# A searched instruction order for chunk-selected attention with a gated MLP: a new order, zero products moved to the front, loads moved, and two gate tiles transposed by TensorE

## The chip, the core and the metric

The kernel runs on one core of one Trainium2 chip. The metric is the device time of one execution in microseconds (us). The engines are TensorE (PE, with its weight loads shown apart as PEld), VectorE (DVE), ScalarE (ACT), GpSimd (POOL) and SyncE (SP). In this kernel POOL issues all loads from memory, and SP issues all other DMAs: copies inside the chip's memory, transpositions by DMA, and the stores of the output.

## The reference

For each of 4 batches and 8 heads (768 positions, head size 64), each query picks at most 6 of 24 key chunks of 32 by an upper bound, attends to those causally, and the result goes through a gated MLP. Cut to what is computed:

```python
k_min, k_max = k_chunks.min(axis=3), k_chunks.max(axis=3)
ub  = sum(maximum(q * k_min, q * k_max), -1)          # bound of each query with each chunk
sel = the 6 chunks with the largest ub among the causal ones
scores = where(sel & causal, q @ k.T / 8, -1e9)
x   = softmax(scores) @ v                             # heads side by side: [4, 768, 512]
h   = relu(x @ w_in);  u, v = h[..., :512], h[..., 512:]
v_n = (v - mean(v)) / sqrt(var(v) + 1e-6)
out = (u * (w_spatial @ v_n + b_spatial)) @ w_out
```

## The kernel before

**Tiles and stages.** Positions are six tiles of 128. Two heads make a pair: pairs 0 to 15, four to a batch. Two pairs make a group, 0 to 7, which is what one load of K, Q or V covers. For each pair the kernel transposes keys and queries on PE, reduces the keys to chunk bounds on DVE, multiplies bounds with the positive and negative parts of the queries, takes the 8 largest per query and head, and writes the mask of what is not selected beside the queries. Queries and mask are transposed together, so that one product gives masked scores. ACT takes the exponential, PE multiplies with V, DVE divides by the sum. When a batch's four pairs are done its MLP runs, and PE mixes its products with the attention of the next batch. After the last pair only the MLP of batch 3 is left.

**The order.** Every piece of work has a name. One long string, `ORDER` (L379 on), lists all 1446 names, and the kernel's last loop emits them in that order. Each engine runs its own pieces in the order in which they are emitted and waits where an operand or a buffer is not ready. The string came from a planner in the same file (`Sim` and `build`), which has a cost and a priority for each piece; it isn't run when the kernel is, except that `build(PLAN)` says which engine takes which piece. `PLAN['flip']` lists pieces that go to the other of ACT and DVE.

**Names used below.** With `i` a pair, `g` a group, `h` one of two heads and `b`,`t` a batch and a token tile:

- `dz`, `dm0` to `dm64`: a cleared tile (L564) and 65 products of it with itself (L868), which nobody reads; they keep PE busy while the first data is on its way.
- `ring0` to `ring3`: clearing of the query buffers (L527); `id0`, `id1`: the identity matrix (L523, L524); `kh..`: clearing halves of the key operands (L569).
- `lk`, `lq`, `lv` with g and h: loads of K, Q, V (L584, L590, L595; group 0 by head and pair, L599); `win`, `wsp`, `wout`, `lb`: MLP weights (L603 to L622).
- `kT`, `qT`: transposes of keys and queries (L660, L717); `kTb0`, `kTb1`, `qTb0`: a second copy of them for the first pairs; `kc`: the copy of a transposed key out of PSUM (L698); `kop`: the key operand, a copy by DVE or ACT, and from pair 8 on a DMA on SP (L710).
- `kmax`, `kmin`, `kb`: key bounds (L681, L703); `rq`: query parts (L726, L728); `ub`: the bounds' product; `top`, `sel`: selection (L747, L773).
- `aT`, `ac`: transposes of query and mask on PE and their copy (L792, L795); from pair 8 on `aTd` does this by DMA on SP (L798).
- `sc`, `ex`, `tri`, `av`, `rc`, `nm`: scores (L805), exponentials (L814), the causal triangle on POOL (L820), values product (L831), reciprocal (L836) and division (L841); `x`, `xp`: transposition of the result, from pair 4 on by DMA (L850).
- MLP: `v`, `u`, `s`, `o` products (L925, in halves `.0`, `.2`, `.4`), `va`, `ua` relus, `bs`, `vs`, `rs`, `vn` the normalisation, `gt` the gate (L968), `gd` its transposition by DMA (L974), `oc` the copy of an output tile out of PSUM (L979), `os` its store (L983).

**What sets the order around the change.** `av000` needs `lv0`; `qT2` needs `lq10` and `lq11`. A score needs `aT`/`aTd` and `kop` of its pair. An output tile `o` needs the transposed gate tile of `gd`. PSUM has three banks for scores, three for MLP products, and one each for transposes (`tr`) and values.

The lines of the transposition by DMA are

```python
st["gT", ti] = ml.tile([P, KO, P], F16, tag="gT", name="gT", bufs=NQT)
nc.sync.dma_start_transpose(out=st["gT", ti], in_=st["g", ti])
```

Of the kernel before, what the change touches and what calls it, by code (L numbers as in the profile page):

```python
# [59 lines left out]
class Sim:  # L60
# [10 lines left out]
    def run(s,fixed=None):  # L71
# [16 lines left out]
        warm=getattr(s,'warm0',0.) or 1e9; touch={}  # L88
# [8 lines left out]
        while n<N:  # L97
# [68 lines left out]
def mmc(n): return max(n/2.4+2.5,25)/1000  # L166
DEF=dict(BEATS=12,pa=8,dve_a=(),qx=('ACT',),xp=4,mlp_first=13,mlp_mul=1.0,sc=3,tr=1,acc=1,ml=3,kbuf=3,qbuf=3,vbuf=3,ebuf=3,late=240,chunk=2,
  lk=40,lq=36,lv=18,kdma=99,kcp=2,kcdma=1,kc_act=(),shift=4,prep=0.0,tm=0.0,lm=0.0,head=1,lag=0.0,kp=27,ca=99,tree=0,svk=1.4,svw=1.15,flip=(),wide=0,pt=(),xd=(),dum=0,warm0=0.,qa_dve=(),ma_act=(),mkbuf=2)
PEL=0.2
def build(prm=None):  # L170
# [24 lines left out]
    for g in range(1,8):  # L195
        t0=2*g*BE
        for hi in range(2):
            op(f'lk{g}{hi}','POOL',1.007,acq=[('k',g)],prio=t0-p['lk']+hi,dma=(p['svk'],1.9+p['lm']))
            op(f'lq{g}{hi}','POOL',1.007,acq=[('qs',g)],deps=[f'ring{g}'] if g<p['qbuf'] else [],prio=t0-p['lq']+hi,dma=(p['svk'],1.9+p['lm']))
        op(f'lv{g}','POOL',1.41,acq=[('v',g)],prio=t0-p['lv'],dma=(2*p['svk'],1.9+p['lm']),deps=['small'])  # L200
# [120 lines left out]
    for b in range(B):  # L321
# [29 lines left out]
        for ti in range(NQT):  # L351
            op(f'vn{b}{ti}','DVE',.457,.09,deps=[f'rs{b}'],acq=[('vn',b)],uses=[('vraw',b)],prio=pri[last('u',b,ti,4)]+.6)
            q=pri[last('s',b,ti,6)]
            op(f'gt{b}{ti}','DVE',.66,.09,deps=[last('s',b,ti,6),f'ua{b}{ti}','lb'],acq=[('g',f'{b}{ti}')],uses=[('ml',f's{b}{ti}'),('u',b)],prio=q+.5)
            op(f'gd{b}{ti}','SP',1.22,deps=[f'gt{b}{ti}'],acq=[('gT',f'{b}{ti}')],uses=[('g',f'{b}{ti}')],prio=q+.7,dma=(.82,1.5+p['tm']))
# [21 lines left out]
PLAN = {'late': 40, 'mlp_first': 8, 'qbuf': 4, 'kbuf': 4, 'vbuf': 4, 'dum': 65, 'warm0': 6.5, 'kcp': 8, 'flip': ['ac11', 'ac20', 'ac60', 'kc11', 'kc9', 'kh11', 'kh20', 'kh21', 'kh30', 'oc00', 'oc02', 'oc11', 'oc13', 'oc14', 'oc15', 'oc22', 'oc24']}  # L377

ORDER = """  # L379
ring3 lk010 ring1 dz lq010 ring0 dm13 dm14 dm55 dm31 dm7 id0 dm11 ring2 lk000 dm59 dm53 dm20 dm27 dm4 small dm46 dm42  # L380
dm23 lq000 dm1 dm50 dm60 dm61 dm35 dm22 dm25 id1 dm40 dm47 dm63 lk011 dm39 expand lk001 kh20 kh00 kh21 lq001 kh30 kT0
kh11 dm57 dm3 dm52 dm64 kTb0 kmin0 lq011 dm8 dm36 qT0 kop01 dm30 qTb0 rq00 lk10 dm5 dm9 dm6 dm28 dm15 dm24 kmax0 rq01
dm10 dm37 dm41 dm26 dm48 dm18 dm19 dm43 dm21 dm51 dm33 mlat kop00 kT1 kb0 lk11 dm17 dm45 kmax1 kh31 kTb1 lv0 dm58 ub0
kmin1 dm32 kop11 dm38 dm0 dm44 dm54 dm12 dm62 qT1 dm34 dm29 top00 kh10 mtri rq11 kh01 top01 lq11 selA0 kb1 aTA00 sel0
kop10 dm16 rq10 dm56 dm2 aTB0 lq10 acA00 ub1 acB0 aTA01 sc000 top10 lk20 sc001 ex000 dm49 acA01 kT2 top11 sc002 ex001
win11 sc010 kop20 ex002 sc003 win30 kop21 ex010 av000 sel1 lq21 sc004 ex003 kmax2 sc005 aT11 ex004 sc011 win31 kmin2
aT10 ex005 ex011 lq20 av001 sc013 ac10 av002 ac11 sc015 sc012 rc00 lk21 qT2 kb2 ex013 nm00 qT3 ex015 kT3 rq20 ex012
sc100 win10 rq21 sc102 ex100 av010 rq30 lk30 sc014 kmax3 ex102 sc101 ub2 ex014 lq30 sc103 kmin3 ex101 av011 sc111
ex103 lv1 av012 top20 sc112 ex111 sc105 rc01 top21 ex112 sc104 nm01 ex105 lk31 sc114 ex104 kb3 rq31 sc113 av100 sel2
ex113 sc110 win21 kop31 aT20 ex114 kop30 ub3 win20 aT21 ex110 ac20 av101 sc115 top30 av102 ex115 sc200 ac21 sc203  # L390
top31 lq31 sc201 rc10 sel3 kT4 ex200 nm10 qT4 ex203 lq40 sc204 kmax4 av110 ex201 sc202 ex204 av111 kmin4 sc215 aT30
win01 ex202 xp0 sc205 ex215 rq40 sc211 ac30 kb4 sc210 kop40 av112 lv2 ex205 ex211 rq41 sc212 kop41 ex210 ub4 sc213 x0
ex212 kT5 rc11 sc214 top40 ex213 sc300 ex214 nm11 aT31 sc301 top41 ex300 av200 lq41 kop50 ex301 av201 sc305 sel4 sc302
ac31 kmin5 av202 qT5 win00 xp1 ex305 ex302 sc310 rq50 sc303 lk40 rc20 ex310 rq51 sc304 nm20 ex303 aT40 sc311 kmax5
wsp0 ex304 av210 sc315 ex311 av211 kop51 sc312 ac40 av212 x1 kT6 ex312 rc21 sc313 kb5 nm21 aT41 ex315 ex313 kmax6
sc405 xp2 ac41 av300 sc314 x2 av301 ex405 sc404 ex314 kmin6 sc400 ub5 ex404 sc401 av302 top50 ex400 sc403 kT7 rc30
ex401 top51 sc402 ex403 sel5 nm30 aT50 ex402 sc415 kmax7 av310 ac50 sc411 tri40 av311 sc412 kb6 ex415 kop61 qT6 ex411
wsp2 av312 sc413 ex412 rq60 sc410 wsp3 rc31 ex413 rq61 sc501 wsp4 nm31 ex410 aT51 wsp5 sc503 kop60 av400 ac51 lk50
kmin7 sc414 xp3 ex501 ub6 x3 av401 ex503 sc502 av402 top60 ex414 v00.0 rc40 ex502 sc504 kb7 nm40 v00.2 tri41 ex504
sc505 top61 sc500 av410 ex505 wsp1 sel6 ex500 sc511 av411 kop70 qT7 lv5 sc514 kop71 av412 sc510 ex514 rq70 v02.0 rq71  # L400
va00 v01.0 lk41 ex510 aT60 bs00 v01.2 ex511 lv4 ac60 v02.2 va01 rc41 sc513 nm41 ub7 va02 v03.0 top70 ex513 lb sc603
sc515 v04.0 bs01 ex515 ex603 v03.2 tri50 top71 av500 vs01 va03 vs00 v04.2 bs02 av501 sc601 va04 sel7 av502 sc512 ex601
aT61 rc50 bs03 sc600 ex512 wsT0 bs04 wsT1 ac61 tri51 v05.0 wsc0 ex600 sc605 sc602 nm50 aT70 lv3 v05.2 vs04 vs02 ac70
wsc1 av510 wsT2 ex605 kT8 va05 wout2 wsc2 sc613 ex602 av511 lk51 bs05 sc604 av512 ex613 u01.0 kc8 ex604 sc610 u01.2
kmin8 ex610 kop80 sc611 tri60 sc612 ua01 x4 u00.0 kmax8 ex611 qT8 lq50 u00.2 ex612 vs03 rq80 sc614 sc703 ua00 rc51
lk71 wsT4 nm51 ex614 wsT3 rq81 u02.0 ex703 lq51 vs05 kb8 aT71 wsc4 rs0 u02.2 wsc3 ac71 wsT5 vn03 sc704 sc700 vn01
av600 ex704 ub8 vn00 ex700 av601 u03.0 wsc5 ua02 sc702 vn05 u03.2 ex702 u04.0 top80 ua03 av602 top81 sc705 sc710 u04.2
ex705 rc60 ex710 nm60 kT9 ua04 sel8 sc615 sc701 u05.0 vn02 aTd8 ex615 ex701 av610 kmin9 tri61 s00.0 sc714 kmax9 sc711
tri70 av611 ex714 x5 sc712 av612 ex711 qT9 vn04 wout3 s00.2 kc9 rc61 lv6 rq91 u05.2 nm61 ex712 sc713 s00.4 kb9 ua05
rq90 av700 s01.0 gt00 ex713 ub9 av701 gd00 s01.2 top90 s02.0 top91 av702 sc800 kop81 kT10 rc70 ex800 nm70 s01.4 kop90  # L410
sel9 s02.2 x6 gt01 sc801 av710 ex801 sc715 kmin10 qT10 s02.4 aTd9 ex715 sc804 tri71 s03.0 gt02 ex804 sc803 av711
kmax10 wout0 s03.2 ex803 gd01 wout1 av712 s04.0 rq100 sc802 rc71 rq101 sc805 kop91 sc810 ex802 s04.2 kb10 kc10 gd02
s03.4 ex810 nm71 sc813 ex805 ub10 gt03 ex813 sc812 tri80 x7 av800 ex812 s05.0 top100 kT11 top101 sc811 sc814 kmin11
av801 ex811 s05.2 ex814 av802 sel10 sc815 s05.4 rc80 ex815 aTd10 nm80 s04.4 tri81 sc905 sc901 gt04 av810 ex905 ex901
sc900 lk61 sc902 gd03 kmax11 qT11 ex900 av811 o00.0 ex902 lk60 rq110 sc911 kc11 sc910 kop101 gt05 av812 sc904 kop100
lq61 ex910 o00.2 rc81 kop111 o02.0 ex911 oc00 o01.0 kop110 lq60 ex904 kb11 o02.2 nm81 sc903 o01.2 oc02 x8 ex903 av900
rq111 v10.0 oc01 tri90 v11.0 gd04 av901 v10.2 lq71 av902 sc913 va10 sc912 os00 sc915 v13.0 bs10 ex915 gd05 ex913 ub11
v11.2 top110 v12.0 va11 rc90 sc914 nm90 v13.2 bs11 v14.0 va13 v12.2 vs10 top111 ex912 v14.2 sel11 va12 o03.0 vs11 bs13
va14 sc1004 av910 ex914 kT12 bs14 sc1000 ex1004 o03.2 tri91 kc12 ex1000 av911 sc1001 kmax12 v15.0 kop120 oc03 sc1002
ex1001 aTd11 qT12 kmin12 u10.0 v15.2 vs14 bs12 av912 u10.2 os01 va15 rc91 sc1003 os03 ex1002 u11.0 bs15 ex1003 sc1012  # L420
o04.0 rq121 ua10 nm91 u11.2 sc1005 vs15 o04.2 kb12 ua11 vs12 rq120 kT13 ex1012 sc1010 u12.0 kmin13 ex1010 sc1014 u12.2
ex1005 oc04 kc13 av1000 tri100 sc1011 ex1014 vs13 kmax13 ub12 u13.0 ua12 lq70 sc1015 av1001 rs1 top120 u13.2 vn10
# [32 lines left out]
def kernel(  # L455
# [456 lines left out]
    def mlp(b):  # L912
# [19 lines left out]
        def each(ti):  # L932
# [38 lines left out]
            @act(f"gd{b}{ti}")  # L971
            def gate_dma():
                st["gT", ti] = ml.tile([P, KO, P], F16, tag="gT", name="gT", bufs=NQT)
                nc.sync.dma_start_transpose(out=st["gT", ti], in_=st["g", ti])  # L974
# [54 lines left out]
```

## Time and profile before

| | us |
|---|---|
| three timed runs | 206.35, 205.96, 206.19 (median 206.19) |
| span of the profiled execution | 205.4 |
| the same execution, timed | 207.09 |

| engine | busy us | share of the span | instructions |
|---|---|---|---|
| PE | 189.3 | 92% | 2004 |
| DVE | 159.9 | 78% | 479 |
| ACT | 142.6 | 69% | 287 |
| POOL | 80.2 | 39% | 96 |

The page also cuts the span into 40 slices and gives the busy share of each in tenths, with the share of the DMA engines:

```profile
PE   4767999998999999999979999999999999999972
DVE  6998899999998989999668989697857537387410
ACT  2396999999899986578677868389689552563151
DMA  6999999994999999999999998966895145251565
```

How to read it: a slice is 5.1 us and 9 means 90% or more. PE is full over most of the span and less so in the first five slices, in one slice half way and in the last two. DVE and ACT are near full up to about 55 us and have room later. The granted PE clock is full throughout the page, which is the throttle's share only.

### The profile page before, as it was taken

How to read it: one execution, taken by the hardware profiler on the slowest of the kernel's cores; microseconds unless marked ns; L12 is line 12 of the kernel's file. 1: busy time of each engine (PE TensorE's matmuls, PEld its weight loads, DVE VectorE, ACT ScalarE, POOL GpSimd, SP SyncE). 2: the span in 40 equal slices, each digit the busy share in tenths (PEclk: the TensorE clock that was granted, in tenths of full speed). 3: DMA queues.
4: the chain of work that ended last, by engine and by line, in shares of the span. 5: the costliest groups of instructions: out<-in, count | busy, mean ns of one | idle time of the engine just before them, and what ended most of it. 6: DMA issues, size and time to landing. Idle time of an engine off the chain costs nothing.

```text
span 205.4 us, 5197 instructions
## 1 busy us (share of the span) xinstructions
PE 189.3 (92%) x2004; PEld 118.2 (58%) x2004; DVE 159.9 (78%) x479; ACT 142.6 (69%) x287; POOL 80.2 (39%) x96
## 2 busy tenths in 40 slices
PE   4767999998999999999979999999999999999972
PEld 4765777775667666665535546556555555444430
DVE  6998899999998989999668989697857537387410
ACT  2396999999899986578677868389689552563151
POOL 7998776607777715338310511111603030000000
PEclk9999999999999999999999999999999999999999
DMA  6999999994999999999999998966895145251565
GB/s 42 102 118 147 167 163 162 159 143 58 165 147 93 163 133 164 185 174 129 155 145 188 188 144 199 131 185 134 104 234 131 26 109 86 77 218 44 141 165 203
DMA packets 115706, 28.86 MB, mean 141 GB/s; under 512 B 109793, under 2 KB 112097, under 8 KB 115681
## 3 DMA queue, kind: packets, MB, share of 16 engines
q0 software_dynamic: 76544, 12.20, 86.2%
q1 hardware_dynamic: 39136, 16.33, 38.7%
q8 instruction: 16, 0.26, 0.5%
q14 instruction: 10, 0.07, 0.1%
HBM read 24.38 MB, written 6.29 MB: 149 GB/s over the span
## 4 chain that ended last, share of the span: by engine, by line
PE 60%; DVE 17%; DMA 10%; POOL 4%; ACT 3%; SPq 2%; issue 2%; POOLq 0%; DVEq 0%
PE mlp L925 36%; PE sc L805 11%; PE acc L831 7%; DMA vt<-in_v_dram 4%; DVE kmm L681 4%; DMA kh<-kT 4%; DVE kh L712 2%; DMA gT<-g 2%; DVE max L747 2%; DVE vn L962 2%; DVE x L841 2%; POOL k L599 2%; ACT e L814 2%; SPq L974 2%; POOL qs L599 1%
## 5 line engine op out<-in xcount | busy, mean ns | idle before, releaser
L814 ACT ACTIVATE e<-sc 128x512 f16<-128x512 f32 (+1 forms) x192 | 94.2, 559 | 25.1 <-PE sc L805 21.6
L805 PE MATMUL sc<-a,kh 128*128 128x128 f16 (+3 forms) x256 | 60.7, 305 | 1.7 <-DMA kh<-kT 1.4
L820 POOL TENSOR_SCALAR_AFFINE_SELECT e<-e 128x768 f16<-128x768 f16 x24 | 21.2, 887 | 81.4 <-ACT e L814 60.2
L925 PE MATMUL mlp<-w_in_sb,xT 128*128 128x512 f16 x192 | 52.2, 379 | 0.0
L831 PEld LDWEIGHTS <-e 128*128 128x128 f16 x672 | 31.7, 97 | 14.7 <-issue 1.2
L925 PE MATMUL mlp<-vn,wsT 128*128 128x512 f16 x144 | 39.1, 379 | 0.2
L831 PE MATMUL acc<-vt,e 128*128 128x65 f16 x672 | 36.1, 193 | 1.0 <-DMA vt<-in_v_dram 1.0
L805 PEld LDWEIGHTS <-kh 128*128 128x128 f16 x256 | 23.1, 97 | 15.8 <-DMA kh<-kT 1.9
L681 DVE TENSOR_REDUCE kmm<-kTp 128x24 f16<-128x768 f16 x32 | 29.7, 949 | 0.9 <-PE kTp L660 0.6
L925 PE MATMUL mlp<-w_out_sb,gT 128*128 128x512 f16 x96 | 25.8, 379 | 1.6 <-DMA gT<-g 1.6
L968 DVE SCALAR_TENSOR_TENSOR g<-mlp,b_col,u 128x512 f16<-128x512 f32 x24 | 17.9, 748 | 10.2 <-PE mlp L925 9.5
L925 PEld LDWEIGHTS <-xT 128*128 128x128 f16 x192 | 16.7, 97 | 13.4 <-issue 0.2
L947 DVE BATCH_NORM_STATS2 stats<-vraw 128x6 f32<-128x512 f32 x24 | 16.1, 680 | 8.3 <-ACT vraw L942 8.3
L979 ACT COPY o<-mlp 128x512 f32<-128x512 f32 x16 | 9.2, 587 | 14.3 <-PE mlp L925 14.3
L942 ACT ACTIVATE vraw<-mlp 128x512 f32<-128x512 f32 x24 | 13.8, 600 | 7.4 <-PE mlp L925 7.2
L841 DVE TENSOR_TENSOR x<-acc,rec 128x384 f16<-128x384 f32 x32 | 17.7, 552 | 0.9 <-DMA xT<-x 0.4
L925 PEld LDWEIGHTS <-wsT 128*128 128x128 f16 x144 | 12.4, 97 | 10.2 <-issue 0.8
L957 ACT ACTIVATE u<-mlp 128x512 f16<-128x512 f32 x24 | 14.3, 604 | 5.0 <-PE mlp L925 4.3
L747 DVE MAX8 max<-ub 128x8 f32<-128x8 f32 (+4 forms) x160 | 15.3, 165 | 0.7 <-PE ub L737 0.5
L590 POOL DMA_DIRECT2D qs<-in_q_dram x14 | 14.5, 1036 | 3.2 <-DMA vt<-in_v_dram 2.5
L584 POOL DMA_DIRECT2D k<-in_k_dram x14 | 14.5, 1036 | 0.7 <-DMA k<-in_k_dram 0.4
L962 DVE TENSOR_SCALAR vn<-vraw,mv,rstd 128x512 f16<-128x512 f32 x24 | 13.3, 609 | 1.9 <-ACT rstd L989 1.8
(73 smaller groups left out, 226.4 us busy)
## 6 DMA issues: line engine op xcount, KB each, us to landing
out_dram<-o SPq DMA_DIRECT2D x24, 256.0 KB, 2.9
vt<-in_v_dram POOLq DMA_DIRECT2D x8, 384.0 KB, 7.5
k<-in_k_dram POOLq DMA_DIRECT2D x14, 192.0 KB, 7.3
qs<-in_q_dram POOLq DMA_DIRECT2D x14, 192.0 KB, 8.8
kh<-kT SPq DMA_DIRECT2D x16, 96.0 KB, 4.3
ws_raw<-in_moe_w_spatial_dram POOLq DMA_DIRECT2D x6, 192.0 KB, 4.8
w_in_sb<-in_moe_w_in_dram POOLq DMA_DIRECT2D x8, 128.0 KB, 8.1
w_out_sb<-in_moe_w_out_dram POOLq DMA_DIRECT2D x4, 128.0 KB, 4.1
```

Source lines behind the costliest of these rows:

```text
L584: nc.gpsimd.dma_start(out=k_tile(g)[:, :, :, hi, :].rearrange("p x t d -> p (x t) d"), in_=source(k, b, 2 * hp + 2 * hi, 2))
L681: nc.vector.tensor_reduce(self.kmm[:, m, :], src.rearrange("d (c ch) -> d c ch", ch=CHUNK), axis=AX.X, op=op, negate=(m == 1))
L747: nc.vector.max(self.max8[:, qi - 1, hi, :], self.ub[:, c0:c0 + CPT * (qi + 1)])
L805: mm(sc[:, col:col + n], lhsT=self.kh[hi][:, t * P:(t + 1) * P], rhs=self.a[:, q0 // P:(q0 + n) // P, hi, :], start=True, stop=not diag)
L814: nc.scalar.activation(out=self.e[hi][:, g * 512:g * 512 + width], in_=self.sc[hi, g][:, 0:width], func=Act.Exp, scale=scale)
L820: nc.gpsimd.affine_select(out=blk, in_=blk, compare_op=Alu.is_ge, fill=0.0, base=0, channel_multiplier=-1, pattern=[[0, NQT], [1, P]])
L831: mm(self.av[hi][:, qi, :], lhsT=self.e[hi][:, c:c + P], rhs=self.v[hi][:, t, 0:D + 1], start=first and n == 0, stop=last and n == len(blo ...
L841: nc.vector.tensor_tensor(self.x16[:, :, hi, :], in0=self.av[hi][:, :, 0:D], in1=self.rec[hi].to_broadcast([P, NQT, D]), op=Alu.mult)
L925: mm(st[kind, ti], lhsT=lhsT, rhs=rhs, start=(j == 0), stop=(j == n - 1))
L947: nc.vector.bn_stats(st["stats", ti], st["vraw"][:, ti, :])
L962: nc.vector.tensor_scalar(vn[:, ti, :], in0=st["vraw"][:, ti, :], scalar1=st["mv"][:, ti, 0:1], scalar2=st["rstd"][:, ti, :], op0=Alu.subt ...
L968: nc.vector.scalar_tensor_tensor(g, in0=st["s", ti], scalar=b_col[:, ti:ti + 1], in1=st["u"][:, ti, :], op0=Alu.add, op1=Alu.mult)
```

## The change

The string `ORDER` is replaced by another one of 1448 names, and a few pieces change their engine or their kind. The planner's changes (when a cold clock ends, 0.8 us more landing time for transpositions, 0.2 us for loads up to group 3 and 1.2 us for later ones, and `ring` and `small` behind `id0`) have no effect but through that string. What differs in the kernel that runs:

- `dz` and `id0` are DVE's first operations; before, `ring3` and `ring1` stood ahead of `dz`. Ahead of `kT0` stand 14 of the 65 zero products instead of 25.
- The first loads are lk000, lk010, lq010, lq000 instead of lk010, lq010, lk000, lq000. The loads up to `lv0`, `lq10` and `lq11` keep their places. Later ones move: `lk41`, `lk61`, `wsp3`, `wsp5`, `lv2`, `lq60` go earlier, `lq30`, `lq31`, most of `win`, `lq40`, `lq41`, `lv5`, `lv6` later.
- To ACT go `ac11`, `ac20`, `kc13`, `kc14`, `oc14`, `oc15`, `oc02`, `oc24` and the clears `kh30`, `kh21`, `kh20`, `kh11`; to DVE go `ac21`, `ac71`, `rq01`, `kh31`, `kh01`, `oc01`, `oc12`, `oc20`.
- On SP, `kop81`, `kop90` stand before `gd00`; `kop100` before `gd02`; `kop101` and `kop110` before `gd03`; `aTd10` behind `gd03`; `gd14` far later.
- The gate tiles (3,4) and (3,5) are transposed by four PE transposes into the `tr` bank and copied out, the first by ACT and the second by DVE, instead of by DMA.

```diff
-PLAN = {... 'dum': 65, 'warm0': 6.5, 'kcp': 8, 'flip': ['ac11', 'ac20', 'ac60', 'kc11', 'kc9', 'kh11', 'kh20', 'kh21', 'kh30', 'oc00', 'oc02', 'oc11', 'oc13', 'oc14', 'oc15', 'oc22', 'oc24']}
+PLAN = {... 'dum': 65, 'warm0': 5.3, 'kcp': 8, 'flip': ['ac21', 'ac60', 'ac71', 'gd34', 'kc11', 'kc13', 'kc14', 'kc9', 'kh01', 'kh31', 'oc00', 'oc01', 'oc11', 'oc12', 'oc13', 'oc20', 'oc22', 'rq01'], 'gp': ((3, 4), (3, 5)), 'lm': 0.2, 'lm2': 1.2, 'tm': 0.8}
...
-ring3 lk010 ring1 dz lq010 ring0 dm13 dm14 dm55 dm31 dm7 id0 dm11 ring2 lk000 dm59 dm53 dm20 dm27 dm4 small dm46 dm42
+dz id0 dm50 ring0 dm19 dm26 lk000 dm35 dm14 dm55 dm53 ring1 dm13 dm36 dm49 lk010 dm6 dm1 small dm46 dm60 ring2 lq010
...
-s33.4 gd32 s34.2 gt33 s35.0 s34.4 gd33 s35.2 gt34 o30.0 s35.4 gd34 o31.0 gt35 o30.2 o31.2 gd35 oc30 o32.0 oc31 o33.0
-o32.2 os31 o34.0 os30 oc32 o33.2 o34.2 os32 oc33 o35.0 oc34 os33 o35.2 os34 oc35 os35
+gt33 o30.0 s34.4 s35.0 gd33 gt34 s35.2 o30.2 os25 s35.4 oc30 o31.0 gp34 os30 gt35 o31.2 gd34 o32.0 oc31 o34.0 o32.2
+os31 o33.0 oc32 gp35 o33.2 gd35 os32 o34.2 oc33 o35.0 oc34 os33 o35.2 os34 oc35 os35
...
+            @act(f"gp{b}{ti}")
+            def gate_transpose():
+                st["gp", ti] = ps_tr.tile([P, KO, P], F16, tag="tr", name="gp")
+                for j in range(KO):
+                    nc.tensor.transpose(st["gp", ti][:, j, :], st["g", ti][:, j * P:(j + 1) * P], identity)
+
             @act(f"gd{b}{ti}")
             def gate_dma():
                 st["gT", ti] = ml.tile([P, KO, P], F16, tag="gT", name="gT", bufs=NQT)
+                if (b, ti) in prm["gp"]:
+                    copier(engine[f"gd{b}{ti}"])(st["gT", ti], st["gp", ti])
+                    return
                 nc.sync.dma_start_transpose(out=st["gT", ti], in_=st["g", ti])
```

## Prediction

> **What bounds the kernel now.** I read the page first, then a table by stages of 5 us, then the chain of waits in order of time, then the timeline around each place the change touches. Four stages of the table (stage, its length, busy us of PE, of PE's weight loads, of DVE, ACT and POOL with instruction counts, granted clock, DMA share, GB/s):
>
> ```profile
> 25.00:30.00 5.00, 4.73 (x79) 3.65 (x78) 4.92 (x24) 4.66 (x12) 3.85 (x5) 1.00 2.23 164
> 75.00:80.00 5.00, 5.00 (x61) 3.05 (x58) 5.00 (x12) 4.41 (x10) 3.96 (x4) 1.00 1.62 159
> 100.00:105.00 5.00, 3.52 (x21) 1.33 (x16) 4.09 (x19) 3.35 (x7) 0.66 (x1) 1.00 2.02 178
> 195.00:200.00 5.00, 4.01 (x19) 1.64 (x17) 0.75 (x1) 2.73 (x5) 0.00 (x0) 1.00 0.66 169
> ```
>
> From about 22 to 57 us VectorE (DVE) has nearly no free time. From 57 to 195 us TensorE (PE) is busy in every stage but one. So a gain has to come from the start, from the hole at 100-105, or from the end. The chain of waits names the waits (start, length, what):
>
> ```profile
> 11.27 8.02 DMA vt<-in_v_dram
> ...
> 97.08 0.59 SPq L710
> 97.71 7.30 DMA kh<-kT
> 105.05 0.39 PE sc L805 x2
> ...
> 194.71 1.22 SPq L974
> 196.02 4.37 DMA gT<-g
> 200.44 1.05 PE mlp L925 x4
> 201.51 0.59 ACT o L979
> ```
>
> First: the first values product (`av000`) waits for the V load of group 0. Second: the first score of pair 10 waits for a key operand whose copy was issued only at 97.08. Third: the last output tile waits for the transposition by DMA of the last gate tile. PE's own rows in the timeline give the third hole (start, busy, then in brackets the idle time before it and its releaser):
>
> ```profile
> 194.97 4.05 PE L925 MATMUL mlp<-w_out_sb,gT 128*128 128x512 f16 x18
> 200.44 1.04 PE L925 MATMUL mlp<-w_out_sb,gT 128*128 128x512 f16 x4 [1.42 <-DMA gT<-g]
> ```
>
> SP's queue around the second hole:
>
> ```profile
> 90.48 2.57 SPq L850 DMA_TRANSPOSE xT<-x  x1
> 93.23 1.54 SPq L798 DMA_TRANSPOSE a<-qs  x1
> 94.82 2.21 SPq L974 DMA_TRANSPOSE gT<-g  x1
> 97.08 2.59 SPq L710 DMA_DIRECT2D kh<-kT  x4
> ```
>
> The four key copies of pairs 10 and 11 stand behind three transpositions: SP issues without a pause from 80.66 to 112.5, so its order decides when they land.
>
> **What the Trainium skill says.** DMA: Bandwidth & Descriptors, "Issuing engines are not separate DMA queues": DMAs of SP and GpSimd share the same 16 engines and interleave. The trace agrees: the key copies land 2.0 us after issue at best and 9.1 at worst, and the slow ones are those at 95-100, when POOL loads are in flight. TensorE: Matmul & The Clock Gate, Part 1: PE is at half clock until about 3.4 us of sustained activity. The trace agrees: the first 25 zero products take 2.85 us (114 ns each), 17 later ones 1.22 (72 ns), and from 10.67 six transposes take 0.50. VectorE: DVE Perf Modes, "The three transpose paths": 390 ns for one 128x128 transpose on TensorE against 1309 by DMA. Here six on TensorE take 0.50 us back to back and a gate tile by DMA takes 2.4 to 4.4 us to land, so the measurements are used.
>
> **The change, part by part.**
>
> *Zero products first.* `dz` goes ahead of the two ring memsets (1.51 us from 1.04), so PE starts at about 1.2 instead of 2.67. But only 14 zero products now stand before `kT0` instead of 25, some 1.6 us of work; then PE waits for keys. I see no sure earlier full clock. Nothing is gained that the next point does not cap.
>
> *Start.* `lk010` moves from third to second load; the third landed at 6.57, 2.65 us after its issue ended at 3.92, so `kT0` can run at 3.10+2.65=5.75, 0.8 earlier. DVE loses four key-half clears and `ac11` up to `rc00` (4x0.565+0.554=2.81) and gains two clears and `rq01` (2x0.565+0.472=1.60): 1.2 us less. ACT takes what DVE gives up; it idles 3.67 us before its first copy. So the selection of pair 0 is 0.8 to 1.4 us sooner. But the loads stay where they were: POOL issues without a real gap from 1.32 to 15.2, V of group 0 is still its 11th load and the queries of pairs 2 and 3 its 12th and 13th. V landed at 19.29. The second query load was issued at 14.26 and took 7.8 us: 22.06, and PE's next weight load is `qT2` at 22.16. DVE's `rq` after it began at 22.75; it can begin at 22.65. Therefore about 0.1 us survives. From there DVE does the same operations up to `x3`, except that `kmin7` (0.95) goes behind and `kop70` (0.555) ahead: 0.4 less. I take 0.3 us in all. Bounds: a gain of 1.2, if the DVE time saved carries through, and a loss of 0.5, if the order fits ACT worse (4.66 of 5 busy).
>
> *Loads.* From 20 to 45 us POOL's load queue moves 155-165 GB/s. From the 14th load to `lq31` it now carries 3392 KB instead of 2488, so `lq31` lands at about 22.1+3392/160=43.3; `qT6` is wanted at about 49. `lv1` comes earlier (1856 KB instead of 2048). `lv5` moves from 54.6 to behind `tri90` and `lq70`: issued at about 99.2, landing at 107 (median 7.5) to 111 (worst 11.5), wanted by `av1000` at 113. POOL's triangle masks behind them wait 2 to 8 us for ACT as it is. Cost nothing, hidden by PE's other work.
>
> *Pair 10.* `kop100` is now issued before `gd02` and `x7`, and kop101, kop110 right after: some 6 us sooner, so the wait on the keys goes. But `aTd10`, the transposed query operand, is pushed behind `gd03` and three key copies, and its source `sel10` behind five DVE operations. Issue: 93.23, less 1.23 for `kop81` and `kop90`, which now fill an idle stretch of SP before 80.66, plus 3x0.6, plus 1.24 for `gd03`: 95.0. With the landing it had before (7.1) that is 102.1; with the median (5.0), 100.0. Wanted: the first score of pair 10 reached PE at 105.05-1.37=103.7; av902, sc915, v12.2, v14.2 and o03.0 (about 1.55 us of PE) now come after it: 102.1. So of a stall of 1.37 us between nothing and all remains. I take 0.9 gained. Behind the waiting score stand all of PE's instructions, so a late landing counts in full.
>
> *End.* The transpositions of the last two gate tiles leave SP and DMA; PE gets eight transposes (8x0.057 = 0.46), ACT one copy and DVE one copy of 128x512 from PSUM (nearest rows: 0.59 on ACT, 0.41 on DVE). PE's 18 matmuls need 18x0.2165=3.90, so the hole before `o35` is 200.44-198.87=1.57. `gp34` ends two half-tiles (0.86) before `o34.0`, enough for about 0.2 of latency and ACT's 0.59; `gp35` stands 0.86 before `o35.0`, enough for 0.2 and 0.41. Gain 1.57-0.46=1.1; I take 1.0. Bounds 0.6 and 1.3. The six stores need SP earlier and find it free from about 195; in the trace they run at up to 394 GB/s, 0.7 us for 256 KB, and the output tiles are 0.9 us apart, so the last does not queue.
>
> *The rest.* Flips of `kc13`, `kc14` and output copies between ACT and DVE, and the new order in 57-195, lie beside a full PE: nothing, within 0.3 either way.
>
> Sum: 0.3+0.9+1.0=2.2 us from the span of 205.4. That execution was timed at 207.09; the three runs are at 206.19 (205.96 to 206.35). The difference applied to the median: 204.0.
>
> **Rivals.**
> - *The end alone.* The wait for keys becomes an equal wait for `aTd10`, and the loads swallow the start: 206.19-1.0=205.2. For it: SP and the loads are the limit in both places. Against: with the median landing `aTd10` is there 2 us before it is wanted.
> - *The start carries through.* If the loads land sooner, DVE's 1.2 us is kept: 206.19-1.2-0.9-1.0=203.1. Against: the load queue is unchanged there.
> - *Slower: `aTd10` lands late.* If `gd03` again takes 2.21 to issue and SP's idle stretch is not filled, it goes out at about 97; `x8`, issued at 99.77, took 10.0 us. Landing at 107, the score waits 4.9 us instead of 1.4: +3.5, less 1.0 and 0.3: 208.4. It decides from a landing at 104.7 (1.4+1.3 us after 102.1). For it: SP's full queue. Against: `lk61` and `lq60` now move much earlier, so fewer loads are in flight.
> - *The zero products do not bring the clock earlier*, since PE rests 3 us after them: already in the forecast, 0.
>
> **How the numbers follow.** Forecast 0.50, end alone 0.20, start carries 0.12, slower 0.18. The forecast's own range is 203.2 to 205.0. No change means within 0.2%, 205.78 to 206.60, about what this measurement can tell. Nearly all of the first, most of the second and all of the third are faster: 0.77; same 0.05 (a weak form of the second or fourth); slower 0.18. The range takes in the third case to 203.0 and the second with some of a new stall to 206.2.
>
> **What would show it.** Right: no idle PE before `o35`; `av000` still released by V at about 19.3; `qT2` at about 22.1; the first score of pair 10 waiting under 0.7 us. Wrong: a wait on `a<-qs` of over 2 us near 102, a new DMA wait in 57-195, or DVE's `rq` of pair 2 well before 22.6.

## The result, and the profile after

| | us |
|---|---|
| kernel before, timed | 206.35, 205.96, 206.19 and one of 211.10 |
| changed kernel, timed | 202.85, 203.32, 203.83, 203.78 (median 203.55) |
| ratio of the two | 0.987, 95% interval 0.983 to 0.990 |
| span of the profiled execution, before and after | 205.4 and 201.2 |

The ratio is 2.7 us of 206.2, with 2.0 to 3.4 as its interval. The two profiles differ by more, 4.2 us: the profile of before fell on an execution timed at 207.09, that of after on the shortest of its four. On the chips of the later runs executions of the kernel before alone spread over 205.3 to 213.7 us, so every ratio below is taken of the runs within 1.5% of the fastest of their kernel, and what only the profiles of longer executions show (those with spans of 207.0 us and more) is not put down to the order.

Most lines of the changed kernel are 5 higher than those of before (scores L810, divisions L846, MLP products L930, key copies L715), and at the end 14 higher (transposition of a gate tile L988, output copies L993, stores L997). The gate tiles turned by PE are L980, their copies L986.

The slices of the page, after (5.0 us each):

```profile
PE   3899999999999999999999999999999999999991
DVE  6989999999899999989598968794886547376520
ACT  2879999899799994867588958598799461664052
DMA  6999999999999999999999986959983253150355
```

PE has reached nine tenths from the third slice and keeps it until the last but one; the slice at seven tenths half way and the one before the end are gone. The table by stages of 5 us, after, with the same columns as before:

```profile
25.00:30.00 5.00, 4.76 (x78) 3.81 (x75) 4.93 (x25) 5.00 (x12) 3.25 (x4) 1.00 1.85 162
75.00:80.00 5.00, 5.00 (x76) 3.35 (x74) 4.70 (x16) 2.81 (x6) 2.03 (x3) 1.00 1.19 172
100.00:105.00 5.00, 5.00 (x49) 2.90 (x48) 4.66 (x20) 4.57 (x11) 1.16 (x2) 1.00 2.10 162
195.00:200.00 5.00, 1.78 (x9) 0.59 (x6) 0.42 (x1) 1.68 (x4) 0.00 (x0) 0.90 0.62 236
```

The hole at 100 to 105 (3.52 of 5 busy before) is filled. In the last stage PE has only 1.78 us left to do, since it is done at 196.8. The chain of waits, after:

```profile
14.12 6.79 DMA qs<-in_q_dram
21.04 0.45 PE trq L722 x5
...
76.73 6.23 DMA kh<-kT
...
195.05 1.74 PE mlp L930 x8
196.81 0.59 ACT o L993
```

The V load is no longer in it. The second query load of pairs 2 and 3 has taken its place: it flew 6.79 us and landed at 20.91, not at 22.06. There is no DMA of the last gate tile ahead of the last output products. PE's own rows at the end show why, in the timeline:

```profile
192.72 2.11 PE L930 MATMUL mlp<-w_out_sb,gT 128*128 128x512 f16 x9
194.66 0.39 PE L980 MATMUL gp<-identity,g 128*128 128x128 f16 x4
194.89 1.89 PE L930 MATMUL mlp<-w_out_sb,gT 128*128 128x512 f16 x8
```

No idle time stands before any of the three rows. SP's queue around pair 10, after:

```profile
86.26 0.53 SPq L715 DMA_DIRECT2D kh<-kT  x1
86.83 1.28 SPq L988 DMA_TRANSPOSE gT<-g  x1
88.21 1.38 SPq L855 DMA_TRANSPOSE xT<-x  x1
89.63 1.23 SPq L715 DMA_DIRECT2D kh<-kT  x2
90.96 1.30 SPq L988 DMA_TRANSPOSE gT<-g  x1
94.04 1.82 SPq L803 DMA_TRANSPOSE a<-qs  x1
```

The first key copy of pair 10 goes out at 86.26 instead of 97.08, `gd03` at 90.96 instead of 94.82, and `aTd10` at 94.04. The first score of pair 10 starts at 100.56 without a wait.

**Where the time went, in this pair of profiles.** Two marks on PE cut the span in three: `v00.0`, the first MLP product of batch 0, and `s30.0`, the first spatial product of batch 3. The work of PE ahead of them is the same in both kernels, but for one score product (some 0.2 us) ahead of `v00.0`. The start, to `v00.0`: 52.50 before, 50.74 after, 1.8 us less. The middle, `v00.0` to `s30.0`: 132.97 and 131.18, 1.8 less. The end: 19.91 and 19.23, 0.7 less. Forecast were 0.3, 0.9 and 1.0. Whether the differences are the change's or those of two single executions is the first question for the runs.

### The profile page after: what moved, and what is told of

Same layout as the page of the kernel before. It is cut to its first block, busy times and chain, and to the rows that moved or that the text cites. A ratio compares the mean times of both kernels' runs of the same rounds, so it can differ in the third digit from the quotient of the medians.

```text
span 201.2 us, 5218 instructions
## 1 busy us (share of the span) xinstructions
PE 189.7 (94%) x2012; PEld 119.8 (60%) x2012; DVE 157.4 (78%) x476; ACT 147.4 (73%) x292; POOL 79.7 (40%) x96
## 3 DMA queue, kind: packets, MB, share of 16 engines
q1 hardware_dynamic: 38048, 16.06, 37.4%
## 4 chain that ended last, share of the span: by engine, by line
PE 64%; DVE 15%; DMA 10%; POOL 6%; issue 2%; SPq 1%; ACT 0%; POOLq 0%
PE mlp L930 41%; PE sc L810 11%; PE acc L836 7%; DVE kmm L686 4%; DMA qs<-in_q_dram 3%; DMA a<-qs 3%; DMA kh<-kT 3%; DVE kh L717 2%; DVE max L752 2%; DVE x L846 2%; POOL qs L604 2%; POOL k L604 2%; DVE rq L731 1%; PE trq L722 1%; DVE rq L733 1%
## 5 line engine op out<-in xcount | busy, mean ns | idle before, releaser
L810 PE MATMUL sc<-a,kh 128*128 128x512 f16 (+3 forms) x256 | 61.6, 305 | 0.7 <-DMA kh<-kT 0.2
L930 PE MATMUL mlp<-w_in_sb,xT 128*128 128x512 f16 x192 | 51.9, 379 | 0.0
L930 PE MATMUL mlp<-vn,wsT 128*128 128x512 f16 x144 | 38.8, 379 | 0.1
L810 PEld LDWEIGHTS <-kh 128*128 128x128 f16 x256 | 22.8, 97 | 14.1 <-issue 0.6
L973 DVE SCALAR_TENSOR_TENSOR g<-mlp,b_col,u 128x512 f16<-128x512 f32 x24 | 17.8, 747 | 11.6 <-PE mlp L930 10.8
L930 PE MATMUL mlp<-w_out_sb,gT 128*128 128x512 f16 x96 | 26.4, 379 | 0.0
L930 PEld LDWEIGHTS <-xT 128*128 128x128 f16 x192 | 16.9, 98 | 14.6
L993 ACT COPY o<-mlp 128x512 f32<-128x512 f32 x17 | 9.9, 589 | 14.2 <-PE mlp L930 14.2
L947 ACT ACTIVATE vraw<-mlp 128x512 f32<-128x512 f32 x24 | 14.5, 602 | 5.7 <-PE mlp L930 5.7
L930 PEld LDWEIGHTS <-wsT 128*128 128x128 f16 x144 | 12.5, 97 | 10.1 <-DVE vn L967 0.3
L846 DVE TENSOR_TENSOR x<-acc,rec 128x384 f16<-128x384 f32 x32 | 17.6, 548 | 0.4
L930 PEld LDWEIGHTS <-gT 128*128 128x128 f16 x96 | 8.9, 98 | 8.4 <-ACT gT L986 0.3
```

The costliest lines, as they stand in the source:

```text
L810: mm(sc[:, col:col + n], lhsT=self.kh[hi][:, t * P:(t + 1) * P], rhs=self.a[:, q0 // P:(q0 + n) // P, hi, :], start=True, stop=not diag)
L846: nc.vector.tensor_tensor(self.x16[:, :, hi, :], in0=self.av[hi][:, :, 0:D], in1=self.rec[hi].to_broadcast([P, NQT, D]), op=Alu.mult)
L930: mm(st[kind, ti], lhsT=lhsT, rhs=rhs, start=(j == 0), stop=(j == n - 1))
L973: nc.vector.scalar_tensor_tensor(g, in0=st["s", ti], scalar=b_col[:, ti:ti + 1], in1=st["u"][:, ti, :], op0=Alu.add, op1=Alu.mult)
```

## The experiments

All ratios are to the kernel before, run together with it on the same chip, with 95% intervals. The three stages are those above, read from one profiled execution of each kernel.

| kernel | ratio | V of group 0, issue to landing | `v00.0` starts | middle | end | span |
|---|---|---|---|---|---|---|
| before | 1 | 8.0 | 52.50 | 132.97 | 19.91 | 205.4 |
| `again` | 0.9998 (0.9966 to 1.0029) | 7.8 | 52.05 | 133.17 | 19.89 | 205.1 |
| `kop100_alone` | 0.9986 (0.9955 to 1.0018) | 7.9 | 52.11 | 135.67 | 19.93 | 207.7 |
| `two_dmas` | 0.9958 (0.9911 to 1.0004) | 7.3 | 51.49 | 135.59 | 19.90 | 207.0 |
| `tail_alone` | 0.9975 (0.9937 to 1.0012) | 8.9 | 54.57 | 134.97 | 18.95 | 208.5 |
| `head_alone` | 0.9991 (0.9960 to 1.0023) | 7.3 | 52.31 | 138.35 | 18.75 | 209.4 |
| `head_undone` | 0.9948 (0.9917 to 0.9978) | 7.5 | 52.62 | 131.90 | 18.95 | 203.5 |
| changed kernel | 0.9868 (0.9833 to 0.9904) | 6.8 | 50.74 | 131.18 | 19.23 | 201.2 |
| `after_again` | 0.9879 (0.9792 to 0.9966) | 6.9 | 50.78 | 132.37 | 19.00 | 202.1 |
| `after_third` | 0.9828 (0.9773 to 0.9882) | 6.7 | 50.69 | 132.56 | 19.36 | 202.6 |
| `win_back` | 0.9827 (0.9777 to 0.9877) | 6.4 | 51.06 | 132.04 | 19.18 | 202.3 |
| `sp_undone` | 0.9921 (0.9875 to 0.9967) | 6.7 | 50.86 | 133.24 | 18.93 | 203.0 |
| `early_warm` | 0.9799 (0.9724 to 0.9874) | 6.7 | 50.77 | 131.19 | 18.93 | 200.9 |
| `early_warm_2` | 0.9789 (0.9730 to 0.9847) | 7.5 | 52.79 | 135.79 | 18.93 | 207.5 |

The middle differs most between executions of code that is the same there: it ran from 133.0 to 138.4 us where the order is the old one, and it is longest where the whole span is long. Start and end repeat better. Only the starts of `tail_alone` and `early_warm_2` stand out, and there the granted clock of PE was low (see the last section).

### The two kernels once more

Edit of `again`: none against before.

> The kernel before, unchanged, a second time. It tells how far one profiled execution stands from another. In the two profiles at hand the first values product (av000) came at 19.33 us before and 17.96 us after, the wait ahead of the first score of pair 10 was 1.37 us before and nothing after, and the span differed by 4.2 us where the timed medians differ by 2.7. Theory 'loads vary': the landing of V of group 0 differs between executions of the same code by about a microsecond, so av000 lies anywhere in 17.9 to 19.4 here. Theory 'the order did it': av000 is at 19.3 within 0.3, and the wait of pair 10 is 1.0 us or more again. Time: ratio 1.000.

Edit of `after_again` and `after_third`: none against the changed kernel.

> The changed kernel a second time. Theory 'the middle has more room now': PE's waits between 66 and 125 us stay under 0.5 us together, where kernels with the old order there showed 1.4, 1.8, 5.4, 2.6 and 3.2 us in five executions, and the time is 1.2 to 1.5% below that of the kernel before, 2.5 to 3.1 us. Rival 'one lucky execution': waits of 1.4 us or more between 66 and 125, and a difference of 1.5 us or less. Start: av000 between 17.9 and 18.9, qT2 between 21.0 and 21.8; if the start is worth more than 0.5 us, qT2 lies below 21.2 again. End: no wait ahead of o35.

> The changed kernel a third time, as the companion of the three others: ratio 0.987 within 0.003, v00.0 at 50.8, no wait ahead of o35, PE's waits between 66 and 125 us between 0 and 1.3 us.

Measured: in `again`, `av000` came at 19.14 and the score of pair 10 waited 1.09 us, with another 0.69 us ahead of it for a gate tile. In the three executions of the changed kernel `av000` came at 17.96, 18.12 and 17.89, `v00.0` at 50.74, 50.78 and 50.69, and nothing waits ahead of `o35`. The ratios of the changed kernel are 0.987, 0.988 and 0.983. So the start of the pair of profiles is no accident: between old and new order lies more than between these executions of one order, and "loads vary" does not explain it.

In the middle the first profile of the changed kernel was a lucky one. Two of three have a wait that the first has not, 1.04 us in both. PE's row of `after_third` in the timeline, and those of DVE just before:

```profile
95.63 0.44 PE L722 MATMUL trq<-identity,qs 128*128 128x128 f16 x5 [1.04 <-DVE qs L778]
```

```profile
94.03 0.75 DVE L973 SCALAR_TENSOR_TENSOR g<-mlp,b_col,u 128x512 f16<-128x512 f32 x1 [1.45 <-PE sc L810]
94.69 0.44 DVE L752 MAX8 max<-ub 128x8 f32<-128x20 f32 x4
95.17 0.41 DVE L778 TENSOR_TENSOR qs<-ub,max 128x240 f16<-128x240 f32 x1
```

The selection that fills the query buffer (`sel10`, L778) stands on DVE behind a gate multiplication that waits 1.45 us, and PE's next transposes of queries wait for the end of that. `head_undone` and `win_back`, which have the new order here, show this wait too (1.05 and 0.55 us). It is the place that the prediction named, `sel10` behind five DVE operations, but it was charged there to `aTd10`.

### The end alone

The kernel before, from `s34.2` on with the new order:

```diff
-s34.2 gt33 s35.0 s34.4 gd33 s35.2 gt34 o30.0 s35.4 gd34 o31.0 gt35 o30.2 o31.2 gd35 oc30 o32.0
+s34.2 gt33 o30.0 s34.4 s35.0 gd33 gt34 s35.2 o30.2 s35.4 oc30 o31.0 gp34 os30 gt35 o31.2 gd34 o32.0
...
+PLAN: 'gp': ((3, 4), (3, 5)), and 'gd34' in 'flip'
```

> The kernel before with the end alone changed: from s34.2 on the new order, with gate tiles (3,4) and (3,5) transposed by PE and copied out by ACT and DVE. Prediction: the hole of 1.57 us ahead of o35 goes, 0.46 us of PE is added, 1.0 us gained (bounds 0.6 and 1.3), about 205.2 us. Rival 'the stores take some back': o35 starts 1.1 us earlier but the last store, issued while others are in flight, takes 3.5 us instead of 2.0 to land, 0.5 us gained, about 205.7 us.

Measured: ratio 0.9975, 0.5 us less with an interval of 1.3 less to 0.2 more. In the profile the end takes 18.95 us. Four executions with the old end (before, `again`, `kop100_alone`, `two_dmas`) took 19.89 to 19.93. So 0.95 us is gained here; the ratio alone could not show it. Its PE rows:

```profile
199.90 0.39 PE L980 MATMUL gp<-identity,g 128*128 128x128 f16 x4
200.13 2.32 PE L930 MATMUL mlp<-w_out_sb,gT 128*128 128x512 f16 x10
202.29 0.39 PE L980 MATMUL gp<-identity,g 128*128 128x128 f16 x4
202.51 1.89 PE L930 MATMUL mlp<-w_out_sb,gT 128*128 128x512 f16 x8
```

against this row of `two_dmas`, which has the old end:

```profile
202.04 1.04 PE L925 MATMUL mlp<-w_out_sb,gT 128*128 128x512 f16 x4 [1.42 <-DMA gT<-g]
```

What follows: the transposition on PE removes the hole. From `s30.0` to the end of the last product PE took 16.00 to 16.06 us with the old end and waiting, and 14.85 in all nine executions with the new one: 1.15 to 1.2 us less, as worked out (1.1). The rival is right too: from the start of `o35` to the end of the span took 4.90 to 4.94 us in those four old executions and 5.10 to 5.53 in the nine with the new end, so 0.2 to 0.6 us goes back. The last store has most of it: it landed 2.09 to 2.52 us after its issue instead of 2.01 to 2.03. In the three profiles of the changed kernel the end as a whole gains 0.7 us on average (19.20 against 19.91). One more thing shows in `head_alone`, which has the old end: there the last gate tile landed in time, PE did not wait ahead of `o35`, and its end took 18.75. From `s30.0` to the last product PE took 14.41 us there, 0.44 less than with the new end, which is about what the eight transposes cost. So a transposition by DMA at this place costs nothing or 1.5 us, by execution, and where it costs nothing the old end is as short as the new one.

### The middle: SP's order

`kop100_alone`, the kernel before with one name moved:

```diff
-... kb10 kc10 gd02 ... gd03 ... kop101 ... kop100 ...
+... kb10 kc10 kop100 gd02 ... gd03 ... kop101 ...
```

> The kernel before with one name moved: the copy of the first key operand of pair 10 (kop100) is issued on SP ahead of gd02, x7, aTd10 and gd03 instead of behind them; nothing else changes. Theory 'the keys were what pair 10 waited for': the wait of 1.37 us ahead of its first score goes, 1.0 to 1.4 us gained, about 205.0 us. Rival 'aTd10 takes its place': aTd10 goes out 0.6 us later, at about 93.9, lands at 101 or later, and 0 to 0.4 us is gained. Rival 'given back': the wait goes, but the time is the same because PE waits elsewhere later.

`two_dmas`, the same and `x4` ahead of `kop80`:

```diff
-... rc41 sc513 nm41 ... kop80 ... x4 ...
+... rc41 sc513 nm41 x4 ... kop80 ...
```

> The kernel before with two names moved on SP, nothing else: the transposition of the result of pair 4 (x4) is issued ahead of the key copy kop80, which waits for a key and kept x4 waiting behind it until 67 us, and kop100 ahead of gd02. Theory 'SP's order made the waits of the middle': x4 is issued near 60 us, the division nm60 no longer waits for x4's buffer, the first score of pair 10 does not wait, PE's waits between 66 and 125 us fall to 0 to 1.0 us, and 1.3 to 2.0 us are gained, about 204.5 on a chip where before takes 206.2. Rival 'too many loads in flight': x5, x6 or a gate tile land late as before, waits of 1.4 us or more remain, and 0.5 us or less is gained.

`sp_undone`, the changed kernel with the opposite done to both places:

```diff
-... x4 ... aTd8 kop80 ... kop100 gd02 ... x7 ... kop101 kop110 gd03 aTd10 kop111 ...
+... kop80 x4 ... aTd8 ... gd02 ... x7 ... aTd10 gd03 kop101 kop100 kop111 kop110 ...
```

> The changed kernel with SP's order put back in two places: x4 behind kop80, and aTd10, gd03 ahead of the key copies of pair 10. The loads stay where the change put them. Theory 'SP's order made the waits': x4 goes out near 70 us and lands near 75, DVE waits about 1.5 us for its buffer, PE up to 1 us, and the first score of pair 10 waits 1.0 to 1.5 us: 1 to 2.5 us lost against the changed kernel. Rival 'the loads with more slack made the difference': landings are short, each wait is under 0.5 us, and the time stays within 0.5 us of the changed kernel.

Measured: `kop100_alone` has no wait ahead of the first score of pair 10, so the keys were what it waited for. But the gate tile of `gd03` took the place, and in this execution, 207.7 us long, four waits of 0.3 to 0.7 us that the profile of before did not have came up earlier. Two of PE's rows with a wait, `kop100_alone`:

```profile
85.58 0.45 PE L831 MATMUL acc<-vt,e 128*128 128x65 f16 x9 [0.70 <-DVE x L841]
...
105.92 0.60 PE L925 MATMUL mlp<-w_out_sb,gT 128*128 128x512 f16 x2 [0.62 <-DMA gT<-g]
```

In `two_dmas` `x4` is issued at 57.56 instead of 67.25, and no division waits for its buffer; the score of pair 10 does not wait either. What was left was again `gd03`, worse. PE's row in `two_dmas`, and SP's row of `gd03`:

```profile
104.44 0.60 PE L925 MATMUL mlp<-w_out_sb,gT 128*128 128x512 f16 x2 [2.63 <-DMA gT<-g]
```

```profile
95.59 1.99 SPq L974 DMA_TRANSPOSE gT<-g  x1
```

It gained 0.9 us by the ratio (interval 1.8 less to 0.1 more). In `sp_undone` waits come back (0.98 us for the keys of pair 10, 1.17 us for gate tile (0,5)), but `x4`, issued at 64.70 and not near 70, made nobody wait. By the ratios it stands 0.9 us behind `after_again`, its companion, with overlapping intervals; its middle is 0.7 to 2.1 us longer than in the three executions of the changed kernel.

What a late `x4` or `x5` can cost shows in `head_alone`, where this part is the old order, in an execution of 209.4 us. DVE's rows with a wait:

```profile
75.79 0.56 DVE L841 TENSOR_TENSOR x<-acc,rec 128x384 f16<-128x384 f32 x1 [1.46 <-DMA xT<-x]
...
88.11 0.56 DVE L841 TENSOR_TENSOR x<-acc,rec 128x384 f16<-128x384 f32 x1 [4.50 <-DMA xT<-x]
```

A division can't write its result before the transposition two pairs back has read the buffer. In the profile of before the first of these waited 0.45 us on DVE alone, where it cost PE nothing; here they waited 1.46 for `x4` and 4.50 for `x5`, and PE stood 3.72 us for the second. `x5` had been issued at 78.21, as early as in the profile of before (77.38), but landed after 9.80 us instead of 4.01. That PE waits on account of `x4` or `x5` shows only in the longer executions.

What the moved loads do shows in `sp_undone` too. Its SP queue around pair 10:

```profile
94.03 1.42 SPq L803 DMA_TRANSPOSE a<-qs  x1
95.50 1.58 SPq L988 DMA_TRANSPOSE gT<-g  x1
97.12 2.54 SPq L715 DMA_DIRECT2D kh<-kT  x4
```

This is the sequence of before (`aTd10`, `gd03`, the four key copies, there issued at 93.23, 94.82 and 97.08), at nearly the same times. But `aTd10` landed 3.7 us after its issue instead of 7.1, `gd03` 2.8 instead of 8.2, and the first two key copies 3.3 and 3.8 instead of 7.6 and 7.3; `again` repeats the values of before (7.5, 8.8, 7.5, 7.5). In before POOL issued five loads between 92.2 and 98.2, in `sp_undone` two, at 96.7 and 97.7. So with the loads where the change put them, these transfers take about half the time. Since the rest of the new order differs as well, the loads were not tried alone.

What follows: four DMAs of SP had little room in the old order, `x4`, `x5`, the keys of pair 10, and `gd03`, and which one makes PE wait differs by execution. The new order issues the first 9 us earlier, the keys 11 us and `gd03` 4 us earlier, and `x5` 2 us. PE's waits from 66 to 125 us were 1.5 us in before, 1.8 in `again` and 2.1 in `sp_undone`; in the six executions of similar length with the new order there they were 0.0 to 1.3 us. (In the four longer executions of the old order they were 2.6, 2.6, 3.2 and 5.0.) So "SP's order made the waits" holds for the keys, and moving two of the four is not enough. That the earlier `x4` gains anything is not shown. And "the loads with more slack made the difference" is right in one half: the landings got shorter, but keys that are issued at 97 us still come too late.

### The start: the head, the weight loads and the clock

`head_alone`: the new names up to `av000`, then all others in the old order; `head_undone`: the old ones up to `av000`, then the new order, the end included.

```diff
-ring3 lk010 ring1 dz lq010 ring0 dm13 ... sc003 win30 kop21 ex010 av000
+dz id0 dm50 ring0 dm19 dm26 lk000 ... sc011 kop20 lk30 av000
```

> The new order up to av000 (zero products first, first K loads swapped, work of DVE moved to ACT), the old order after it. Theory of the prediction: V and the second query load land when they did, about 0.3 us gained, 205.9 us, av000 at about 19.3. Rival 'the head carries through': av000 at 18.0, qT2 at 21.0, 1.2 to 1.4 us gained, about 204.9 us. If the head gains at av000 and gives it back before the end, the ratio is 1.000 with av000 at 18.0.

> The old order up to av000, with its loads and its work on DVE, the new order after it. Theory 'the head carries through': av000 at 19.0 or later, qT2 at 21.6 or later, v00.0 0.7 to 1.3 us later than the 50.8 us that four executions of the changed kernel and its variants show, and the end as much later. Theory of the prediction, that 0.3 us of the head survives: v00.0 at 51.1 or below.

Measured: `head_alone` gained 0.2 us by the ratio (interval 0.8 less to 0.5 more), and its `v00.0` came at 52.31, within what the old order gives (51.49 to 52.50, leaving out `tail_alone`). `head_undone` lost the larger part of the gain: its ratio is 0.9948 where `after_third`, made together with it, has 0.9828, 2.5 us apart with intervals that do not touch, and its `v00.0` comes at 52.62, 1.9 us later than in the changed kernel. So the head is worth nothing that the ratio can show before the old order, and 1.9 us before the new one. The rows of DVE between the values product and the first query part of pair 2 tell a part of why, first `head_alone`, then `after_third`:

```profile
20.59 0.56 DVE L795 COPY a<-tra 128x768 f16<-128x768 f16 x1
21.57 0.20 DVE L836 RECIPROCAL rec<-acc 128x6 f32<-128x6 f32 x1 [0.42 <-PE acc L831]
...
22.29 0.48 DVE L726 TENSOR_SCALAR rq<-trq 128x640 f16<-128x640 f16 x1
```

```profile
20.64 0.19 DVE L841 RECIPROCAL rec<-acc 128x6 f32<-128x6 f32 x1
...
21.40 0.48 DVE L733 TENSOR_SCALAR rq<-trq 128x640 f16<-128x640 f16 x1
```

With the old order behind it, DVE still does the copy of `ac11` and then waits for PE, which itself waited 0.69 us for an exponential at 19.95; the query part comes at 22.29, as in `again` (22.32). With the new order both are gone and it comes at 21.40. V landed 0.7 us later in that execution of `head_alone` too (18.51 against 17.85), so how the 0.9 us divides between the two is open. From there DVE is the limit (busy 29.4 us or more of the 30 from 20 to 50 us in the three executions of the changed kernel) and carries the 0.9 us on, and more: `v00.0` came at 50.69 against 52.05 in `again`. In `head_undone` it is PE that DVE waits for: it stands 1.89 us until 22.19, and the query part comes at 23.35.

The other half is the loads: V of group 0 was issued within 0.2 us of the same time everywhere, and flew 7.3 to 8.9 us in six executions with the old head and 6.4 to 6.9 in six with the new head and the new order behind it (7.3 in `head_alone` and 7.5 in `early_warm_2`, both with spans over 207). `win_back` asks whether weight loads behind it did that:

```diff
-... lk20 ... lq20 ... win30 ... win11 ...
+... lk20 win11 win30 ... lq20 ...
```

> The changed kernel with two loads put back: win11 and win30 (MLP weights) are issued right behind lk20, as before, instead of near 32 and 41 us; nothing else changes. In five executions of the old order V of group 0 took 8.0, 7.8, 7.9, 7.3 and 8.9 us from issue to landing, in four of the new one 6.8, 6.9, 6.7 and 6.7, though issued within 0.2 us of the same time. Theory 'the weight loads slowed it': V takes 7.3 us or more, av000 comes at 18.6 or later instead of 17.8 to 18.1, and v00.0 at 51.3 or later instead of 50.8. Rival 'the head did it': V takes 6.7 to 6.9 us and v00.0 stays at 50.8.

Measured: V flew 6.4 us, `av000` came at 17.69, the time is that of `after_third` (0.9827 and 0.9828). The weight loads aren't the reason that V lands earlier. `early_warm` asks whether PE's pace counts:

```diff
+dm65 dm66 ... dm90   (26 more zero products, ahead of kT0; 'dum' from 65 to 91)
```

> The changed kernel with 26 more zero products ahead of kT0, 40 instead of 14, so that PE works without a gap from 1.06 to about 5.4 us, when the first keys land at 5.7; nothing else changes. Theory of the prediction, that the loads cap the start: PE is at full clock from about kT0 on (six transposes in 0.5 us instead of 0.8), the selection of pair 0 comes 0.5 to 0.8 us earlier, but av000 still waits for V until about 18.0, qT2 for its queries until about 21.0, and the time is that of the changed kernel within 0.2 us. Rival 'the pace of PE caps the start': av000 and qT2 come 0.4 us or more earlier and so does the end.

> The changed kernel with 40 zero products ahead of kT0, a second time, now beside the changed kernel in the same call. The first time it measured 0.8% less than the changed kernel, but its profile showed v00.0 at the same 50.8 us and only fewer waits near 90 to 96. Theory 'chance': the ratio equals that of the changed kernel within 0.2%, v00.0 is at 50.8, kT0 starts at half a microsecond less or the same. Rival 'a better kernel': 0.4% or more below the changed kernel.

Measured, PE's rows of `early_warm` in the timeline:

```profile
1.06 4.45 PE L874 MATMUL warm<-idle_op 128*128 128x128 f16 x40 [1.06 <-DVE idle_op L570]
5.92 0.59 PE L666 MATMUL kTp<-identity,k 128*128 128x128 f16 x6 [0.41 <-DMA k<-in_k_dram]
...
17.82 0.44 PE L837 MATMUL acc<-vt,e 128*128 128x65 f16 x9 [0.91 <-DMA vt<-in_v_dram]
```

against the first transposes of `after_third`:

```profile
5.80 0.80 PE L665 MATMUL kTp<-identity,k 128*128 128x128 f16 x6 [3.07 <-DMA k<-in_k_dram]
```

The six transposes take 0.59 us instead of 0.80 and the first score comes at 14.32 instead of 15.30. This agrees with what the Trainium skill states under "TensorE: Matmul & The Clock Gate", Part 1, that about 3.4 us of sustained work bring the full clock: here 4.45 us of zero products stand ahead. But `av000` then waits 0.91 us for V and comes at 17.82, and `v00.0` at 50.77, where it always was. A faster PE gains nothing at the start as long as V lands at 17.8. The time was nevertheless lower than that of the changed kernel both times, 0.9799 against 0.9879 and 0.9789 against 0.9828. The intervals overlap, the one profile of an ordinary span shows no gain but the missing wait at 95 us, and the second one's span was 207.5. Whether this kernel beats the changed one is open; no mechanism for it was found.

## Why the prediction was right, and where it was wrong

The forecast was 204.0 us, the measurement 203.55, inside the narrow range (203.2 to 205.0) too. The sum was 2.2 us; the ratio gives 2.7 (2.0 to 3.4), and the three stages, before and `again` against three executions of the changed kernel, give 1.5 (start), 1.0 (middle) and 0.7 (end): 3.3. With `kop100_alone` and `two_dmas`, which are the same there, the start gives 1.3. The number is in part luck: the start was put too low by about 1 us and the end too high by 0.3, and 203.55 lies as far from the 203.1 of the rival "the start carries through" as from the forecast.

- *Zero products first, 0.* Right, and `early_warm` shows more than was claimed: even a clock that is full when the keys land gains nothing at `av000`.
- *Start, 0.3.* Wrong by 1.0 to 1.2. The step that failed is that "the loads stay where they were", with V landing at 19.29 and the second query load at 22.06, so that "about 0.1 us survives". POOL issued V and those queries only 0.15 us earlier than before (11.12 and 14.12), but they landed 1.2 to 1.4 us earlier: V at about 17.9, the queries at 20.9. Against `again` it is about 1.2 us for V and 0.6 for the queries. The cap itself is real, since `av000` waits 0.3 to 0.9 us for V in five of seven executions with the new order. Only its height was taken from one execution of the old order. The rival "the start carries through", which asked that the loads land sooner, describes what happened; its size, 1.2, fits better. DVE's query part of pair 2 at 21.4 to 21.5 is the sign that had been named against the forecast. Why V lands earlier isn't settled: neither the weight loads behind it nor PE's pace; the order of the first four loads and the work that moved from DVE to ACT were not tried apart.
- *Loads moved, 0.* Right as far as PE's waits for the loads go: `av1000` does not wait for `lv5`, no load makes PE wait between 25 and 195 us in the three profiles of the changed kernel, and `win_back` is not slower. (Up to `lq31` the order of before carries 2688 KB, not 2488, and `lq31` landed at 45.1 instead of 43.3, still in time.) What the term leaves out is that the loads are in flight beside SP's transfers: with the loads moved, those around pair 10 landed in about half the time.
- *Pair 10, 0.9 of 1.37.* Right in mechanism: `kop100_alone` shows that the keys were the wait. `aTd10` went out at 94.04, and at 95.58 and 95.65 in the other two executions (forecast 95.0), landed after 3.8 us where 5.0 to 7.1 had been reckoned, and the score started at 100.56 without waiting, so the rival that it takes the keys' place, and the slower one, fell. But part of the 1.0 us is another thing: I put the rest of the new order in 57 to 195 us at nothing, within 0.3. The failing step is there, and in the reading that a gate tile lands in 2.4 to 4.4 us: those of batch 0 took 4.5 to 9.5 us in the same trace. `again`, with the order of before, waited another 0.69 us for `gd03`, of which the one profile showed 0.2. The wait of 1.0 us behind `sel10` takes part of the gain back.
- *End, 1.0.* The hole and the cost of the transposes were right (1.15 against 1.1). The failing step is that the last store "does not queue": its landing took up to 0.5 us longer, 0.2 to 0.6 us goes back in all, and 0.7 us stays.

The rival "the end alone" fell with the start and the middle. That the change is faster was given 0.77; the ratio's interval excludes no change.

## What to carry to other kernels

A landing time read from one trace isn't a constant: before it is used as a cap on a gain, ask what else would have to stay the same for it, and look at more than one execution. On a queue that issues in order, look for transfers whose source has long been ready but which stand behind an instruction that waits; they have no room left even where the trace at hand shows no wait, and with several such places one or another may cost time in every execution, as in the six of the old order here. Look also at what else is in flight while they fly: here their time to landing halved in the order that has the loads elsewhere. And a part of an order can be worth nothing alone and much together with the next part, so an undo from the finished kernel tells more than the part put into the old one.

## What the runs showed that I had not expected

After the hole of 3.72 us in `head_alone` the granted clock of PE fell. Its table by stages, and that of `two_dmas` around its hole of 2.63 us:

```profile
85.00:90.00 5.00, 1.28 (x18) 1.01 (x18) 1.90 (x4) 0.87 (x2) 0.33 (x1) 0.92 1.47 123
90.00:95.00 5.00, 5.00 (x32) 2.58 (x31) 4.17 (x9) 2.24 (x5) 1.60 (x3) 0.74 0.93 118
95.00:100.00 5.00, 5.00 (x72) 3.43 (x70) 4.51 (x17) 3.54 (x10) 2.33 (x3) 1.00 0.87 154
```

```profile
100.00:105.00 5.00, 2.37 (x12) 0.92 (x11) 3.06 (x11) 2.62 (x6) 0.85 (x1) 0.99 2.61 154
105.00:110.00 5.00, 5.00 (x40) 3.12 (x38) 2.95 (x5) 2.38 (x4) 0.00 (x0) 0.67 1.70 215
```

The third figure from the right is the clock: 0.92, then 0.74 while PE is full, then 1.00. A table by 1 us has 0.50 between 90 and 92 us. In all 14 executions PE had three holes of over 2 us in the middle, these two and one of 2.43 us in `early_warm_2`. Each time the clock stood at half for 3.4 us, from half a microsecond after the hole; after shorter ones in the middle, up to 1.4 us, it never did. As an estimate, 3.4 us at half clock cost 1.7 us of PE's work. So a wait may cost more than its length, and four of the five longer executions have at least one such stretch. The clock also stood at half for 3.4 us at the start of `tail_alone` (0.66 on average from 20 to 25 us) and of `early_warm_2` (0.80), among several waits of about 1 us close together; `kop100_alone` has such waits there and kept its clock. None of this was tested.

And one and the same transposition by DMA, that of the last gate tile with the old end, made PE wait 1.4 to 1.5 us in four executions and not at all in a fifth; those of a result (`x4` to `x14`) took 2.5 to 10.0 us within the profile of before alone. With such a spread, a wait that the profile at hand does not show may still be there in the next execution.
